# The same steps of an attention-and-MLP kernel in another written order

## The chip, the cores and the metric

The kernel runs on one core of a Trainium2 chip. The time is the device time of one launch, in microseconds (us), lower being better; where several runs were made, their median is given. A profiled execution, taken by the hardware profiler, gives the start and length of every instruction on the core's engines: TensorE (PE, with its weight loads as PEld), VectorE (DVE), ScalarE (ACT), GpSimd (POOL) and SyncE (SP), which here issues nearly all DMA transfers.

## The reference

Windowed attention with sink tokens, then a gated MLP. Shapes: 4 batches, 8 heads, 768 positions, head width 64; the MLP has 3072 tokens, width 512, inner width 1536. Inputs and output are float32.

```python
scores = scale * np.matmul(q, k.transpose(0, 1, 3, 2))
keep = (pos[None, :] < 4) | ((rel >= 0) & (rel < 128))     # 4 sinks, a window of 128
a = np.exp(np.where(keep, scores, -1e9) - max);  a = a / (sum(a) + 1e-9)
x = np.matmul(a, v).transpose(0, 2, 1, 3).reshape(B * S, H * D)
out = (np.maximum(x @ w_gate, 0.0) * (x @ w_val)) @ w_out
```

## The kernel before

The whole program is written out as a list of tokens, `ORDER`, and a loop at the end calls one small function for each token. A token is a name and its arguments: `G.0.1.5` is `up(0, 1, 5, 0)`. The order of the tokens is the order of the instructions in every engine's queue; the engines wait for each other through semaphores that follow from the data and from the buffers. There is no other loop over the work, so an order is a schedule.

The attention is done in 16 head pairs i, four to a batch (i = 4b to 4b+3). For each pair:

- `kl.i`, `ql.i` load k and q (384 KB each), for pair 0 in halves (`hk`, `hq`); `v.w.j` loads row block j (128 KB; 14 KB for j = 6) of the values of two pairs (w = i // 2). The values are read in pieces of 64 floats, 256 bytes.
- `kc`, `qc` on POOL, `kC`, `qC` on ACT (for halves `hc` and `hd` on POOL, `hC` and `hE` on ACT, `hD` on DVE) cast them to bf16. `c`, `cA` cast values, `f`, `fA` put the sink rows into them.
- For the first six pairs `TK`, `TQ` (halves: `HK`, `HQ`) turn k and q on TensorE, and copies on ACT (`ka`, `kb`, `qA`, `qB`, `ha`, `hX`) or DVE (`kd`, `ke`, `qa`, `qb`, `hg`, `hx`) bring them back; the later pairs are turned by DMA (`tk`, `tq`), and `od` on POOL copies shifted keys.
- `B` or `S` computes the scores of one of three groups g on TensorE, with 64 rows of the array for each of two heads (the form 64*128 in the profile, L411). For pairs 0 to 3 the mask is added by a matmul (`b`, L404), for the others a multiplication on DVE (`M`) applies it after `E`, the exponential on ACT (L426).
- `Vd` sums the exponentials over the keys on TensorE, in tiles of 32 columns (128*32, L445); `t`, `r`, `s`/`sa`, `R` bring the reciprocals into place (DVE, `sa` on ACT).
- `Va.i.part` is the output product on tiles of 64 columns (128*64, L454), and `x.i.part` on DVE writes its scaled result into `xT`, the MLP's input.

All other matmuls use the whole array (128*128). TensorE's form therefore changes whenever the order goes from one of these four kinds to another.

For each batch b the MLP runs over two column groups g (378 and 390 tokens) and 12 blocks m of the inner width: `G.b.g.m` and `W.b.g.m` (L507, 4 matmuls each) make gate and value, `u` on ACT applies the relu, `h` on DVE multiplies into `hT`. `F.b.t.m0.m1` (L529) is the output product of token tile t over blocks m0 to m1; `y` copies it out on ACT, `o` or `p` store it. `Z.3.5` does the last tile in three pieces. The weights are loaded in six chunks of 512 KB each: `gl.c`, `xl.c` (gate, value; blocks 2c and 2c+1) and `ol.c` (output), into six buffers used in turn; `gc`, `xc`, `oc` on POOL and `gC`, `xC`, `oC` on ACT cast a block (for `oc` a chunk), and a buffer is free again when both of its blocks are cast.

The eight PSUM banks are used as four pairs, given out in the order of the tokens by `take`, which picks the free pair that was used longest ago; a pair is free when the last user named has come (`use`). `N.n` and `P.n` (`spin4`, `spin`) are matmuls on zeros at the start that keep TensorE running while the first loads land. The order before does this from its first weights on:

```
S.4.1 gc.4 S.4.0 gc.5 x.2.0 E.4.0 Va.3.0 gC.2 R.3 x.3.0 Va.2.1 x.2.1 Va.3.1 xc.5 x.3.1 gl.0 S.4.2 G.0.0.4 E.4.2
G.0.0.2 E.4.1 xc.4 u.0.0.4 G.0.0.5 kl.5 u.0.0.2 u.0.0.5 gl.5 W.0.0.5 G.0.1.5 W.0.0.4 gc.3 M.4.1 gl.4 xC.2 h.0.0.5 xl.5
```

Lines that the change and the prediction touch:

```python
    30	ORDER = """
    93	F.3.3.8.12 y.3.4 y.3.3 o.3.2 o.3.3 o.3.4 Z.3.5
   578	        for token in ORDER:
   579	            name, *args = token.split(".")
   580	            OPS[name](*map(int, args))
```

Of the kernel before, what the change touches and what calls it, by code (L numbers as in the profile page):

```python
# [40 lines left out]
W.0.0.2 G.0.1.2 xC.0 gC.0 h.0.0.2 u.0.1.5 h.0.0.4 u.0.1.2 gc.11 W.0.1.2 v.3.1 W.0.1.5 h.0.1.2 xC.1 G.0.1.4 u.0.1.4  # L41
xc.3 v.2.0 gC.10 G.0.1.0 gc.9 G.0.1.3 h.0.1.5 W.0.1.4 u.0.1.0 W.0.1.0 h.0.1.0 u.0.1.3 G.0.0.3 G.0.0.11 xc.10 ql.5
W.0.0.3 h.0.1.4 kC.5 W.0.1.3 gC.1 TK.5 u.0.0.3 h.0.0.3 xl.4 G.0.0.0 h.0.1.3 kl.7 xl.3 ke.5 W.0.0.0 xC.11 u.0.0.11
W.0.0.11 qc.5 G.0.1.11 TQ.5 ka.5 h.0.0.11 G.0.1.1 v.2.6 gl.3 qb.5 qa.5 u.0.0.0 gC.8 ol.2 h.0.0.0 W.0.1.11 ql.6 W.0.1.1
S.5.2 u.0.1.1 u.0.1.11 h.0.1.11 xC.9 S.5.0 h.0.1.1 S.5.1 G.0.1.10 ol.5 E.5.2 M.4.2 G.0.0.8 M.5.2 E.5.0 E.5.1 W.0.1.10
G.0.0.10 G.0.1.9 W.0.1.9 xC.8 gc.6 u.0.1.10 xC.6 gc.7 u.0.1.9 W.0.0.10 u.0.0.10 h.0.1.9 h.0.1.10 G.0.0.1 kl.6 xc.7
oc.2 ol.1 h.0.0.10 W.0.0.1 ol.3 G.0.0.9 G.0.1.8 u.0.0.1 h.0.0.1 u.0.0.9 G.0.0.6 qc.6 u.0.0.8 ol.0 W.0.0.9 tq.6 oc.0
ql.7 W.0.0.8 ol.4 h.0.0.8 kC.6 tk.6 G.0.1.7 h.0.0.9 u.0.0.6 M.5.0 G.0.1.6 W.0.1.6 v.2.4 oC.1 M.5.1 W.0.0.6 W.0.1.8
u.0.1.6 h.0.0.6 G.0.0.7 h.0.1.6 oC.3 W.0.0.7 u.0.0.7 v.3.5 kc.7 u.0.1.7 M.4.0 cA.2.0.2 W.0.1.7 u.0.1.8 qc.7 oc.5
h.0.1.7 v.2.2 h.0.0.7 tk.7 Vd.4 Vd.5 v.3.4 od.6 t.2 tq.7 v.2.5 oC.4 v.2.3 od.7 F.0.0.0.8 F.0.1.0.8 S.6.1 h.0.1.8 v.3.0  # L50
# [566 lines left out]
```

## Time and profile before

| | |
|---|---|
| runs (3) | 243.02, 243.04, 244.06 us; median 243.04 |
| the profiled execution's own time | 243.59 us |
| its span, first to last instruction | 241.8 us |
| TensorE busy | 235.4 us, 97% |
| DVE, ACT, POOL busy | 132.4, 131.5, 57.4 us |
| gate and value products (L507) | 144.2 us of matmuls, 768 recorded |
| output product of the MLP (L529) | 60.7 us, 265 recorded |
| scores, sums, outputs of the attention | some 13.5, 10 and 12.1 us |
| HBM read and written | 28.43 and 6.29 MB |

A row of the profile's groups gives the line of the kernel, the engine, the operation, what it writes and reads, the shape, the number of instructions, their busy time, the mean of one, and the idle time of the engine ahead of them with what ended it. The ends of matmuls are modelled and overlap the next start, so the step from start to start is the time that a matmul takes in a stream. A few matmul records can be missing.

### The profile page before, as it was taken

The page shows a single profiled execution, that of the slowest core. Times are in us where ns is not written, and L with a number is a line of the kernel's source. Part 1 is how long each engine was busy: PE and PEld are TensorE (multiplying, and loading weights), DVE is VectorE, ACT ScalarE, POOL GpSimd, SP SyncE. Part 2 cuts the span into 40 slices and gives each one's busy share as a digit, 9 for nine tenths or more (in the row PEclk, how much of TensorE's full clock was granted, in tenths as well). Part 3 has the DMA queues.
Part 4 walks back from the last instruction along what each step waited for, and adds up shares of the span by engine and source line. Part 5 has one row for each costly group of instructions (what it writes and reads, how often), then busy time and mean ns, then how long its engine had stood idle before and what let it go on. Part 6 is the DMA issues. An engine that isn't in the chain of part 4 may idle for free.

```text
span 241.8 us, 4953 instructions
## 1 busy us (share of the span) xinstructions
PE 235.4 (97%) x1916; PEld 136.2 (56%) x1927; DVE 132.4 (55%) x268; ACT 131.5 (54%) x254; POOL 57.4 (24%) x106
## 2 busy tenths in 40 slices
PE   8999899999999999999999999999999999999995
PEld 2656556665546566556555565556574456655444
DVE  6599744737478635366888425397768034443100
ACT  2799877776495243596681163868650342432212
POOL 5467623323428043160103210230000000000000
PEclk9999999999999999999999999999999999999999
DMA  5999999999999999933986927140000180000033
GB/s 166 329 288 298 351 354 290 341 305 250 213 204 227 168 225 194 225 69 86 269 151 162 265 77 154 31 134 0 3 0 3 39 309 1 3 0 0 0 133 130
DMA packets 88327, 38.97 MB, mean 161 GB/s; under 512 B 73712, under 2 KB 83824, under 8 KB 88304
## 3 DMA queue, kind: packets, MB, share of 16 engines
q1 hardware_dynamic: 88160, 38.59, 64.4%
q8 instruction: 15, 0.25, 0.5%
q10 hardware_dynamic: 144, 0.07, 0.1%
q14 instruction: 8, 0.07, 0.1%
HBM read 28.43 MB, written 6.29 MB: 144 GB/s over the span
## 4 chain that ended last, share of the span: by engine, by line
PE 85%; DMA 5%; issue 5%; SPq 1%; ACT 1%; POOL 0%; DVE 0%; POOLq 0%
PE pp L507 52%; PE pp L529 21%; PE pp L454 3%; PE pp L411 3%; DMA ws<-in_moe_w_gate_dram 3%; DMA qf<-in_q_dram 2%; PE pp L445 2%; PE pp L189 2%; SPq L244 1%; PE pp L404 1%; PE pp L369 0%; ACT ee L426 0%; POOL qn L261 0%; PE pp L336 0%; ACT wg L277 0%
## 5 line engine op out<-in xcount | busy, mean ns | idle before, releaser
L519 DVE TENSOR_TENSOR hT<-gs,pp 128x378 bf16<-128x378 f32 (+1 forms) x96 | 50.7, 552 | 73.4 <-PE pp L507 51.6
L514 ACT ACTIVATE gs<-pp 128x378 f32<-128x378 f32 (+1 forms) x96 | 44.2, 494 | 53.9 <-PE pp L507 41.5
L507 PE MATMUL pp<-xT,wg 128*128 128x378 bf16 (+1 forms) x384 | 72.3, 326 | 0.4 <-ACT wg L277 0.4
L507 PE MATMUL pp<-xT,wv 128*128 128x378 bf16 (+1 forms) x384 | 71.9, 325 | 0.0
L529 PE MATMUL pp<-wo,hT 128*128 128x512 bf16 x265 | 60.7, 379 | 1.2 <-issue 1.0
L507 PEld LDWEIGHTS <-wv 128*128 128x128 bf16 x384 | 37.3, 98 | 25.3 <-issue 0.4
L507 PEld LDWEIGHTS <-wg 128*128 128x128 bf16 x384 | 36.8, 98 | 26.1 <-issue 1.0
L426 ACT ACTIVATE ee<-pp 128x1010 bf16<-128x1010 f32 (+2 forms) x48 | 44.0, 961 | 11.9 <-PE pp L411 11.7
L529 PEld LDWEIGHTS <-hT 128*128 128x128 bf16 x276 | 26.1, 98 | 30.4 <-issue 0.4
L535 ACT COPY ws<-pp 128x512 f32<-128x512 f32 x23 | 13.1, 590 | 26.8 <-PE pp L529 26.8
L432 DVE TENSOR_TENSOR ee<-ee,msk 128x1014 bf16<-128x1014 bf16 (+2 forms) x36 | 24.6, 716 | 3.3 <-ACT ee L426 2.9
L490 DVE STREAM_TRANSPOSE R<-r 128x832 f32<-128x832 f32 x16 | 16.4, 1037 | 5.2 <-ACT r L482 4.7
L496 DVE TENSOR_TENSOR xT<-pp,R 128x390 bf16<-128x390 f32 (+1 forms) x32 | 16.1, 543 | 3.9 <-PE pp L454 3.5
L269 POOL CAST vn<-vf 128x512 bf16<-128x512 f32 (+1 forms) x18 | 12.6, 721 | 23.1 <-DMA vf<-in_v_dram 23.1
L411 PE MATMUL pp<-qT,kE 64*128 64x255 bf16 (+4 forms) x164 | 13.5, 248 | 0.3 <-ACT qT L362 0.2
L454 PE MATMUL pp<-ee,vn 128*64 128x252 bf16 (+6 forms) x256 | 12.1, 242 | 0.0
L261 POOL CAST qn<-qf 128x768 bf16<-128x768 f32 x11 | 9.1, 828 | 12.7 <-DMA qf<-in_q_dram 12.4
L454 PEld LDWEIGHTS <-vn 128*64 128x64 bf16 x256 | 10.7, 110 | 1.8 <-issue 1.1
L297 POOL COPY kO<-kE 128x372 bf16<-128x372 bf16 x10 | 5.6, 563 | 25.5 <-PE pp L411 22.9
L258 POOL CAST kn<-kf 128x768 bf16<-128x768 f32 x11 | 9.0, 826 | 8.3 <-DMA kf<-in_k_dram 6.8
L465 DVE STREAM_TRANSPOSE t<-pp 128x832 f32<-128x832 f32 (+1 forms) x10 | 8.7, 868 | 4.2 <-PE pp L445 4.1
L411 PEld LDWEIGHTS <-kE 64*128 64x128 bf16 x164 | 6.8, 93 | 7.2 <-issue 5.1
(89 smaller groups left out, 140.8 us busy)
## 6 DMA issues: line engine op xcount, KB each, us to landing
vf<-in_v_dram SPq DMA_DIRECT2D x48, 128.0 KB, 4.2
kf<-in_k_dram SPq DMA_DIRECT2D x15, 384.0 KB, 5.3
qf<-in_q_dram SPq DMA_DIRECT2D x15, 384.0 KB, 5.7
out_dram<-ws SPq DMA_DIRECT2D x10, 512.0 KB, 3.4
ws<-in_moe_w_gate_dram SPq DMA_DIRECT2D x6, 512.0 KB, 6.4
ws<-in_moe_w_val_dram SPq DMA_DIRECT2D x6, 512.0 KB, 7.6
ws<-in_moe_w_out_dram SPq DMA_DIRECT2D x6, 512.0 KB, 5.1
out_dram<-ws SPq DMA_DIRECT2D x3, 256.0 KB, 2.0
```

Of the source, the lines that this page charges most:

```text
L269: copy(dst[:, j0:j1, :, :].rearrange("p j h d -> p (j h d)"), src[:, j0:j1, :, :].rearrange("p j h d -> p (j h d)"))
L411: mm = lambda h, c0, c1, lhs, rhs, st: on(("S", i, g), "PE", 1 << h, nc.tensor.matmul(out=ps[:, h, c0:c1], lhsT=lhs, rhs=rhs, start=st, st ...
L426: on(("S", i, g), "ACT", 3, nc.scalar.activation(ee[i % NE][:, g, :, 0:n], use(("S", i, g))[:, :, 0:n], Act.Exp, bias=0.0, scale=scale))
L432: nc.vector.tensor_tensor(x, x, msk[:, g, 0:n].unsqueeze(1).to_broadcast([128, 2, n]), op=Alu.mult)
L454: on(("V", i), "PE", 1 << part, nc.tensor.matmul(out=ps[64 * h:64 * h + 64, part, o0:o0 + c1 - c0], lhsT=vn[w % NVN][:, j, h0 + h, :], rhs ...
L490: nc.vector.transpose(out=R[:].rearrange("p s (c e) -> p (s c) e", e=32), in_=r.rearrange("p s c -> p (s c)").unsqueeze(2).to_broadcast([1 ...
L496: on(("V", i), "DVE", 1 << part, nc.vector.tensor_tensor(xT[b % 2][:, p, c0:c1], use(("V", i))[:, part, 0:c1 - c0], held_r[i][:, part, 0:c ...
L507: on(("F", b, g, m), "PE", 1 << which, nc.tensor.matmul(out=ps[:, which, 0:c1 - c0], lhsT=(wg, wv)[which][:, ko, m * 128:(m + 1) * 128], r ...
L514: on(("F", b, g, m), "ACT", 1, nc.scalar.activation(x[:, 0:n], use(("F", b, g, m))[:, 0, 0:n], Act.Relu, bias=0.0, scale=1.0))
L519: on(("F", b, g, m), "DVE", 2, nc.vector.tensor_tensor(hT[:, m, c0:c1], gs[b, g, m][:, 0:c1 - c0], use(("F", b, g, m))[:, 1, 0:c1 - c0], o ...
L529: on(name, "PE", 1 << t % 2, nc.tensor.matmul(out=ps[:, t % 2, :], lhsT=hT[:, m, t * 128:(t + 1) * 128], rhs=wo[:, m, :], start=m == 0, st ...
L535: on(name, "ACT", 1 << t % 2, act_copy(staged(b, t), use(name)[:, t % 2, :]))
```

## The change

Only `ORDER` is rewritten. The steps are the same except for which engine does some of the casts and copies: 53 of 1039 tokens are replaced by tokens for the same step on another engine, and `N.10` by `N.9`. The sequence of forms on TensorE is another (for instance `Va.0.0 Va.0.1 Va.1.0` together, and `Vd.10 Vd.11` together), the loads are asked for in another order, and `v.1.5`, `v.1.3`, `v.1.4` now all stand ahead of `gl.2`, which `xl.2`, `gl.1`, `xl.1`, `xl.0` follow. The core of the diff, the beginning and the stretch of the first MLP tiles and of the output weights:

```diff
 ORDER = """
-hk.0.0 sF sE N.10 sM hk.0.1 hq.0.0 mk.0 hc.0.0 mk.1 mk.2 hq.0.1 sI mb.1 b.0.1 mb.0 HK.0.0 hE.0.0 HQ.0.0 b.0.0 mb.2 P.3
-hD.0.1 kl.1 ql.1 v.0.0 v.0.6 hc.0.1 HK.0.1 kl.2 ql.2 HQ.0.1 v.0.2 ha.0.0 hx.0.0 hX.0.1 hg.0.1 B.0.0 b.0.2 B.0.1 B.0.2
...
-v.1.0 qB.3 t.0.1 B.2.1 r.0.1 v.1.2 b.3.0 b.3.2 kd.3 f.0.5 s.0.1 ke.3 qc.4 E.2.1 B.3.0 Vd.2 R.1 E.3.0 B.3.2 t.1.2 r.1.2
-c.1.0.2 gl.2 c.1.2.4 Va.0.0 E.3.2 f.1.3 Va.0.1 b.3.1 v.1.5 B.3.1 TK.4 v.1.4 TQ.4 Va.1.0 x.0.1 sa.1.2 gl.1 E.3.1 f.1.1
-x.0.0 c.1.4.7 f.1.5 qA.4 R.2 kb.4 x.1.0 Vd.3 t.1.3 P.2 r.1.3 ka.4 xl.2 xl.1 qB.4 Va.2.0 xl.0 Va.1.1 v.2.1 sa.1.3 x.1.1
-S.4.1 gc.4 S.4.0 gc.5 x.2.0 E.4.0 Va.3.0 gC.2 R.3 x.3.0 Va.2.1 x.2.1 Va.3.1 xc.5 x.3.1 gl.0 S.4.2 G.0.0.4 E.4.2
-G.0.0.2 E.4.1 xc.4 u.0.0.4 G.0.0.5 kl.5 u.0.0.2 u.0.0.5 gl.5 W.0.0.5 G.0.1.5 W.0.0.4 gc.3 M.4.1 gl.4 xC.2 h.0.0.5 xl.5
...
+sF sE hk.0.0 sI N.9 sM hq.0.0 hk.0.1 mk.0 mb.0 hq.0.1 mk.2 P.3 hC.0.1 kl.1 hc.0.0 ql.1 mk.1 HK.0.0 v.0.6 mb.1 b.0.0
+hd.0.1 kc.1 hD.0.0 HQ.0.0 HK.0.1 HQ.0.1 v.1.6 ql.2 kl.2 qc.1 P.2 b.0.1 kc.2 mb.2 v.0.3 hg.0.0 hX.0.0 hx.0.1 hg.0.1
+qc.2 B.0.0 b.0.2 E.0.0 B.0.2 B.0.1 TK.1 b.1.1 E.0.2 kd.1 TQ.1 v.0.0 qb.1 qa.1 kl.3 b.1.2 E.0.1 Vd.0 kb.1 B.1.2 v.0.2
+ql.3 v.1.2 kc.3 B.1.1 t.0.0 b.1.0 v.0.5 r.0.0 TK.2 c.0.2.4 B.1.0 kd.2 E.1.2 v.0.4 TQ.2 E.1.1 b.2.2 E.1.0 b.2.0 qa.2
+B.2.0 kl.4 ke.2 qc.3 c.0.4.7 f.0.5 Vd.1 v.0.1 s.0.0 qB.2 E.2.0 f.0.3 TK.3 v.1.1 v.1.0 B.2.2 kb.3 ql.4 t.0.1 b.3.2 R.0
+kd.3 TQ.3 b.2.1 c.0.0.2 E.2.2 f.0.1 kc.4 B.2.1 c.1.0.2 qA.3 qB.3 b.3.0 B.3.2 B.3.0 r.0.1 s.0.1 v.1.5 b.3.1 v.1.3 E.2.1
+f.1.1 R.1 Vd.2 qc.4 B.3.1 E.3.2 E.3.0 c.1.2.4 Va.0.0 Va.0.1 t.1.2 v.1.4 r.1.2 f.1.3 x.0.0 Va.1.0 x.0.1 gl.2 TK.4 E.3.1
+Vd.3 c.1.4.7 sa.1.2 kb.4 x.1.0 t.1.3 R.2 ka.4 xl.2 TQ.4 qA.4 f.1.5 Va.1.1 qB.4 Va.3.0 gl.1 Va.2.0 r.1.3 x.1.1 sa.1.3
+S.4.0 gc.4 gc.5 x.2.0 S.4.1 xc.4 E.4.0 xl.1 R.3 xl.0 kl.5 Va.2.1 Va.3.1 gc.2 S.4.2 x.3.0 xc.2 v.2.6 gl.0 x.2.1 G.0.0.4
+E.4.1 G.0.0.5 xC.5 x.3.1 G.0.1.5 M.4.1 u.0.1.5 W.0.1.5 xc.3 ql.5 W.0.0.5 h.0.1.5 gC.3 G.0.1.2 kc.5 u.0.0.5 h.0.0.5
+W.0.0.4 xl.4 u.0.1.2 gc.1 E.4.2 W.0.1.2 gl.5 G.0.1.4 h.0.1.2 gc.0 G.0.0.3 u.0.0.4 u.0.0.3 G.0.0.2 xc.0 xl.5 u.0.1.4
+gl.3 xc.1 gc.11 qC.5 u.0.0.2 xc.11 W.0.1.4 h.0.0.4 xC.9 TK.5 M.4.2 ke.5 W.0.0.2 W.0.0.3 h.0.1.4 h.0.0.3 gl.4 G.0.1.3
...
+kl.7 ol.5 G.0.1.11 u.0.1.3 u.0.1.0 h.0.0.0 G.0.0.11 u.0.0.11 h.0.1.3 xc.7 v.2.1 ol.3 kl.6 gc.8 W.0.0.11 ol.1 u.0.1.11
+W.0.1.11 G.0.1.1 ql.6 gc.9 h.0.1.0 gc.7 W.0.1.1 h.0.0.11 G.0.1.10 u.0.1.1 h.0.1.11 h.0.1.1 ol.0 S.5.2 E.5.2 S.5.1
+S.5.0 ol.2 W.0.1.10 E.5.1 G.0.0.1 u.0.1.10 W.0.0.1 G.0.0.8 u.0.0.1 W.0.0.8 E.5.0 kc.6 G.0.0.10 h.0.0.1 u.0.0.8 M.5.1
+ql.7 G.0.1.8 u.0.1.8 M.5.0 W.0.0.10 h.0.0.8 tk.6 G.0.1.9 W.0.1.9 u.0.1.9 M.5.2 oC.4 W.0.1.8 qc.6 h.0.1.10 G.0.1.7
...
 """.split()
```

More of the change, by code (lines that the diff above doesn't have):

```diff
@@ L41 @@
[L41 to L50, printed above, removed]
@@ new lines @@
+E.7.0 f.3.3 fA.2.1 M.7.2 ql.8 Va.5.0 M.7.0 M.7.1 v.4.0 c.3.0.2 Va.4.0 R.4 Va.4.1 y.0.2 y.0.3 Va.5.1 Vd.6 cA.3.4.7 Vd.7
+F.0.4.0.8 t.3 kl.10 f.3.1 f.3.5 v.5.2 x.4.0 F.0.5.0.8 Va.7.0 x.4.1 r.3 sa.3 x.5.1 Va.6.0 x.5.0 R.6 ql.10 Va.6.1 R.7
+qc.8 kl.9 kc.8 Va.7.1 F.0.5.8.12 x.7.1 y.0.5 x.6.1 F.0.4.8.12 G.1.1.11 tq.8 x.7.0 G.1.1.4 x.6.0 kc.9 y.0.4 v.5.3
+G.1.0.9 u.1.1.4 W.1.1.4 W.1.1.11 u.1.1.11 G.1.1.5 h.1.1.11 u.1.0.9 u.1.1.5 h.1.1.4 W.1.0.9 G.1.0.0 G.1.1.3 W.1.1.5
+v.4.1 W.1.1.3 W.1.0.0 v.4.3 h.1.1.5 u.1.0.0 G.1.0.7 W.1.0.7 ql.9 u.1.0.7 h.1.0.9 cA.4.0.2 h.1.0.7 ql.11 h.1.0.0
@@ new lines @@
+u.1.1.3 G.1.0.4 h.1.1.3 G.1.1.10 W.1.1.10 u.1.0.4 qC.9 kl.12 G.1.1.8 G.1.1.9 tk.8 u.1.1.9 W.1.1.9 W.1.0.4 v.4.2
+W.1.1.8 u.1.1.10 u.1.1.8 od.8 c.5.2.4 tq.9 h.1.0.4 tk.9 h.1.1.10 G.1.1.7 u.1.1.7 od.9 v.5.1 G.1.0.2 h.1.1.8 G.1.1.0
+W.1.1.7 W.1.1.0 W.1.0.2 h.1.1.9 u.1.1.0 u.1.0.2 h.1.1.7 h.1.1.0 S.8.2 S.8.1 S.8.0 v.5.0 qc.11 h.1.0.2 kC.10 v.5.4
+E.8.1 E.8.0 E.8.2 G.1.0.11 v.5.6 W.1.0.11 G.1.0.10 v.5.5 G.1.1.2 kl.11 tq.11 tk.10 W.1.0.10 u.1.0.11 W.1.1.2 u.1.1.2
+h.1.0.11 qc.10 tq.10 c.4.2.4 u.1.0.10 h.1.0.10 S.9.2 M.8.2 h.1.1.2 E.9.2 S.9.1 S.9.0 G.1.1.1 E.9.0 G.1.0.1 ql.12
@@ new lines @@
+Va.14.0 sa.7 Va.13.0 x.13.0 Va.13.1 x.12.1 x.13.1 x.12.0 Va.15.0 Va.14.1 R.15 R.14 Va.15.1 x.14.1 F.2.4.0.8 x.14.0
+F.2.2.0.8 F.2.5.0.8 x.15.0 F.2.5.8.12 G.3.0.4 x.15.1 u.3.0.4 W.3.0.4 G.3.0.5 h.3.0.4 F.2.2.8.12 u.3.0.5 G.3.1.1
+W.3.0.5 F.2.3.0.8 h.3.0.5 y.2.2 W.3.1.1 u.3.1.1 F.2.3.8.12 y.2.5 h.3.1.1 G.3.1.0 G.3.1.8 y.2.3 F.2.4.8.12 G.3.1.4
+u.3.1.8 p.2.0 y.2.4 W.3.1.8 W.3.1.0 G.3.1.2 W.3.1.4 u.3.1.2 u.3.1.0 p.2.1 W.3.1.2 h.3.1.0 G.3.0.10 h.3.1.8 h.3.1.2
+G.3.0.3 u.3.0.10 G.3.0.1 W.3.0.1 u.3.1.4 u.3.0.3 W.3.0.3 u.3.0.1 h.3.0.1 G.3.0.0 W.3.0.10 h.3.0.3 u.3.0.0 h.3.1.4
@@ L94 @@
+F.3.3.0.8 F.3.3.8.12 y.3.4 o.3.4 y.3.3 o.3.3 Z.3.5
 """.split()
```

77 lines of the change are left out of this document (31 added, 46 removed).

## The prediction

> **What bounds the kernel now.** I read the page first, then TensorE's waits, its timeline around the first gate product, the chain of waits, and ACT's timeline in the same place.
>
> ```profile
> span 241.8 us, 4953 instructions
> PE 235.4 (97%) x1916; PEld 136.2 (56%) x1927; DVE 132.4 (55%) x268; ACT 131.5 (54%) x254; POOL 57.4 (24%) x106
> PE   8999899999999999999999999999999999999995
> ```
>
> TensorE is busy 97%; every other engine has room. A busy share can hide waits, so the waits of TensorE after 27.97 us come next:
>
> ```profile
> PE pp L529 <- issue: 1.0, 6, 0.2
> PE pp L507 <- ACT wg L277: 0.4, 1, 0.4
> ```
>
> The six "issue" gaps are not idle time: the page has 276 weight loads of L529 and only 265 matmuls, and before each such gap one load stands without its matmul. The records are missing, the array was working. So after 27.96 TensorE never waits, and this part of the time is a plain sum of matmuls. Only two things can change it: what a change of tile form costs, and new waits. What lies ahead of 27.96 is another matter:
>
> ```profile
> 26.46 0.35 PE L411 MATMUL pp<-qT,kE 64*128 64x255 bf16 x6
> 26.75 0.81 PE L507 MATMUL pp<-xT,wg 128*128 128x378 bf16 x4
> 27.96 1.55 PE L507 MATMUL pp<-xT,wg 128*128 128x378 bf16 x8 [0.40 <-ACT wg L277]
> ```
>
> G.0.0.4 starts at 26.75 and holds TensorE 0.64 us (the step from tile to tile in the steady part), so G.0.0.2 could start at 27.39. It starts at 27.96: 0.57 us lost (0.40 by the modelled ends). The chain says to what:
>
> ```profile
> 20.30 6.97 DMA ws<-in_moe_w_gate_dram
> 27.26 0.02 issue
> 27.29 0.63 ACT wg L277
> 27.91 0.05 issue
> ```
>
> G.0.0.2 needs the second gate chunk (gl.1), issued at 20.30, landed at 27.26, cast by ACT (gC.2). So the present kernel is a prologue, bound by loads and by ACT, whose useful end is 27.96 - 0.64 = 27.32, and then an unbroken TensorE stream.
>
> **The forms.** A change of form is seen in start times:
>
> ```profile
> 113.84 1.44 PE L507 MATMUL pp<-xT,wv 128*128 128x378 bf16 x8
> 115.22 0.28 PE L411 MATMUL pp<-qT,kE 64*128 64x253 bf16 x2
> ...
> 115.94 0.90 PE L445 MATMUL pp<-ee,ones 128*32 128x127 bf16 x32
> 116.77 1.04 PE L529 MATMUL pp<-wo,hT 128*128 128x512 bf16 x3
> ```
>
> Two W tiles take 2 x 0.64 = 1.28 us in the stream; here 115.22 - 113.84 = 1.38, so entering the score form costs 0.10. Two sums (L445, 128*32) followed by one another step 0.38 each; 116.77 - 115.94 = 0.83, so leaving costs 0.07. By the same subtraction everywhere: sums to outputs (128*64) 0.09, outputs to sums 0.08, outputs to full 0.08, full to sums or outputs 0.09. I counted the changes in both orders along TensorE's queue from G.0.0.4 on: 44 before, 40 after. Three fewer sums to outputs, and one fewer each of outputs to sums, outputs to full and full to sums; one more each of sums to full and full to outputs. Sum: 3 x 0.09 + 0.08 + 0.08 + 0.09 - 0.08 - 0.09 = 0.35 us less, all on the path. Ahead of G.0.0.4 it is 30 against 29, beside waits, so nothing.
>
> **The first weights.** Before, gl.2 is the 25th load and gl.1 has v.1.5 and v.1.4 ahead of it. After, two more value loads (256 KB together) stand ahead of gl.2, and then come xl.2, gl.1, xl.1. TensorE uses gl.2 for three tiles (G.0.0.4, G.0.0.5, G.0.1.5), then xl.2 for two, and needs gl.1 only with the sixth tile, 3.2 us after the first. So gl.1 stops being the gate; gl.2 is. What two value loads cost:
>
> ```profile
> 16.00:18.00 2.00, 2.00 (x22) 1.06 (x21) 1.91 (x9) 1.98 (x5) 2.00 (x5) 1.00 1.05 243
> 24.00:27.00 3.00, 2.68 (x52) 2.13 (x48) 2.86 (x6) 2.33 (x7) 2.33 (x4) 1.00 1.01 344
> ```
>
> The last column is GB/s: 243 while mostly values move, 344 while weights alone do. 0.262 MB at 243 is 1.1 us. The median weight load of a gate takes 6.4 us to land; gl.2 was issued at 17.84, so now it lands at 17.84 + 1.1 + 6.4 = 25.3. Its casts gc.4 and gc.5 (0.61 each, POOL) end at 25.9 and 26.5, in time for a G.0.0.4 at 26.4 and a G.0.0.5 at 27.1. The ends: before, gc.4 started at 25.62 without waiting, so gl.2 had landed by then; plus 1.1 is 26.7 at the latest, or 24 at the earliest. xl.2 takes gl.1's place in bytes (27.26): cast 27.9, wanted at 28.4. gl.1 takes xl.2's (28.5, from the wait that ended at 28.56): cast 29.2, wanted at 29.7. Both fit with 0.5 us.
>
> The Trainium skill, "DMA: Bandwidth & Descriptors", Specifications, speaks against this part: pieces under 512 B do not move at line rate. The values are read in pieces of 256 B, and the two rows agree with it (243 against 344). By byte count at 344 the two loads would have cost 0.8 us, by the rule the 1.1 of the row.
>
> **What sets G.0.0.4 then.** S.4.2 follows E.4.0, and G.0.0.4's last matmul needs x.3.0.
>
> ```profile
> 18.96 1.78 ACT L426 ACTIVATE ee<-pp 128x1010 bf16<-128x1010 f32 x2 [0.17 <-PE pp L411]
> 20.91 0.84 ACT L482 COPY r<-r 32x13 f32<-32x13 f32 x4 [0.18 <-DVE r L470]
> 25.39 1.02 ACT L426 ACTIVATE ee<-pp 128x1010 bf16<-128x1010 f32 x1
> ```
>
> From E.1.0 (14.10) to the end of E.4.0 (26.41) ACT is nearly solid: its steps, plus about 0.8 us of waits (0.17 and 0.18 as shown, with the 0.1 of overlap that each breaks, and two of 0.1 at E.2.2 and E.2.0). After, ka.2 leaves ACT ahead of E.1.0, which can start when E.1.1 lets it, 13.65; qB.2 (0.38) and kb.3 (0.42) come in. Adding the measured steps of the new queue (E 0.90, 0.92 or 0.75 by width, query copies 0.38, r's copies 0.86, key copies 0.42 and 0.51) gives 12.19 us, so E.4.0 ends at 25.84 with no wait, at 26.4 if as much is waited as now. I take 26.1: the scores now come in the order in which ACT reads them, but kl.2 lands behind ql.2, so TK.2 moves from 12.19 to 12.8. G.0.0.4 follows 0.34 us after E.4.0, as now: 26.2 to 26.75, and not before 26.37 by DVE (R.3 after sa.1.3, 1.04, then x.3.0 0.55, wanted 0.48 after G starts). Take 26.5: 0.8 us earlier than 27.32. One spin fewer (0.43 at the cold pace of 427 ns a matmul) saves nothing: TQ.1 waits for qc.1 and so for ql.1, landed at 9.37, in both.
>
> **New waits in the stream.** The old order is tight: some fifteen times after 28 us TensorE starts a tile within 0.2 us of the copy or multiply that frees its bank (G.0.0.8 0.10 after E.5.2, G.2.0.10 0.06 after E.14.0, both net of the 0.05 of a semaphore). The new order has as many such places, others (G.0.0.10 behind E.5.0, G.1.1.2 behind E.8.0, S.9.0 behind h.1.0.10). Each can cost 0 to 0.1; I allow 0.1 in all, ends 0 and 0.8. Two queues are passed by moved steps. On SP, xl.4 now stands ahead of gl.5, xl.5, gl.3, gl.4 and xl.3, and waits for the buffer that xc.3 frees, at about 31.1 (xl.1 lands at 29.82, then gc.2's turn is over and xc.2, xc.3 take 0.6 each); until then kl.5, gl.0 and ql.5 (1.3 MB, 3.8 us at 344) are still moving behind xl.0 (31.21), so the transfers do not stop, and gl.5 lands near 38, wanted cast at 40.2. On POOL, kc.5 stands ahead of gc.1 and gc.0 and waits for kl.5: its place in bytes lies 0.4 of the way from xl.0 (31.21) to the old kl.5 (33.98), 32.3; cast 33.1, TK.5 wants it at 34.3. Both are hidden by over 1 us; gone, each us of lateness is one of TensorE's. ACT, DVE and POOL do the same work in sum, a few casts change engine, and all are at 24 to 55%.
>
> Sum: -0.8 - 0.35 + 0.1 = -1.05 us. The profiled run took 243.59 (span 241.8, 1.79 around it), so it would be 242.5; the median of the runs shown is 0.55 lower, 243.04, and I forecast from it: 242.0.
>
> **Rivals.** *The first weights gate as before.* gl.1 needed 3.0 us more than the value load ahead of it (24.24 to 27.26) for 512 KB; if gl.2, now in that place, does the same, gc.4 ends at 27.9 and G.0.0.4 starts at 27.95, 0.63 late: 243.04 + 0.63 - 0.35 = 243.3. Against it, gl.2 itself did not drag before.
>
> *The prologue closes up fully*: ACT waits for nothing, no new waits: G.0.0.4 at 26.37 or a little under, 243.04 - 0.95 - 0.35 = 241.7, and 241.3 if DVE's chain moves up with the earlier sums.
>
> *Slower: the output weights come late.* ol.2 is now asked for last of the six, and F.0.0.0.8 needs it with its fifth matmul, 34.5 us after G.0.0.4, at 61.0; before, the last was ol.4, which F.0.0.0.8 does not read. At the place in bytes before, ol.0 landed at 57.5; 256 KB more makes 58.4, the cast (1.04) 59.4. If the transfers from 44.63 on (the landing of xl.3, 4110 KB ahead of ol.2's place) run at the 233 GB/s of the stretch from 54 to 60 instead of 313 to 340, those 4.2 MB land at 62.7, the cast ends at 63.7, and TensorE stands 2.7 us: 244.7. It decides from a landing after 60.0.
>
> *Many small waits*: 0.8 instead of 0.1: 242.7.
>
> *The clock.* TensorE's clock was granted from 6.96 us: the steps are 427 ns for 512 columns before, 216 after. If the changed start (spin, then products that wait for casts) lets it come one stretch later, the some 2.7 us of matmuls up to TQ.1 double; 0.6 of it falls into present waits, leaving 2 us: 244.0. The Trainium skill, "TensorE: Matmul & The Clock Gate", Part 1, says the clock opens after a busy window of some 3.4 us that runs free, and one spin fewer speaks against the change by that rule. But in the rows TensorE is solid from 1.06 on, and by the landings it stays so, which is why this gets little.
>
> **Chances.** Forecast (241.6 to 242.4) 0.52; first weights gate 0.15; prologue closes up 0.16; small waits 0.06; output weights 0.08; clock 0.03. About 0.5% (1.2 us, so 241.8 and 244.3) can be told from no change here. Faster: the 0.16 and some 0.22 of the forecast's 0.52, 0.38. Slower: output weights and part of the clock, 0.10. The rest, 0.52, is within. The range for 8 in 10 goes from 241.1 (prologue closed up, with 0.2 for the median) to 243.7 (first weights gate, with some small waits).
>
> **What would show it.** Right: no TensorE wait on wg at L507 or only a trace of it, G.0.0.4 at 26.2 to 26.8 followed at once by five tiles; 40 changes behind it; from it to the last product 0.35 us less. The step on the first weights is wrong if the chain still has a DMA of w_gate just ahead of the first product; the step on ACT if E.4.0 ends after 26.5; the one on new waits if TensorE's waits after 28 us, missing records apart, exceed 0.3 us.

## The result, and the profile after

The changed kernel takes 244.01 us (median of 22 runs, 243.14 to 245.43); the kernel before took 243.33 in as many runs beside it (242.67 to 244.06). The ratio is 1.0033, with a 95% interval of 1.002 to 1.0046: a little slower, above the range of the prediction. The three runs from whose median, 243.04, the forecast was made lie 0.3 us under the median of the 22. The profiled execution took 243.85, with the same span as before.

From the page of the changed kernel:

```profile
span 241.8 us, 4948 instructions
PE 233.9 (97%) x1914; PEld 135.2 (56%) x1926; DVE 131.9 (55%) x274; ACT 127.6 (53%) x242; POOL 61.2 (25%) x112
PE   8798999999999999999999999999999999999994
```

By this row TensorE is busy 1.5 us less, and the span is the same. Some ten matmul records are missing in each page (e2 and e1 below have all 1927 and 1926, and 235.4 and 235.0 us), so the row can't be read that finely. TensorE's waits in the changed kernel after 27 us:

```profile
PE pp L552 <- ACT ws L535: 0.7, 1, 0.7
PE pp L529 <- issue: 0.2, 1, 0.2
```

The second is a missing record. The wait on the gate weights (L507 on wg, 0.4) is gone, and a wait has come up at L552, which is `Z.3.5`, the last tile of the kernel. The timeline of the changed kernel there (start, length, engine, line, operation):

```profile
235.46 0.59 ACT L535 COPY ws<-pp 128x512 f32<-128x512 f32 x1 [1.03 <-PE pp L529]
236.10 2.81 PE L552 MATMUL pp<-wo,hT 128*128 128x256 bf16 x36 [0.67 <-ACT ws L535]
```

and of the kernel before:

```profile
236.12 2.81 PE L552 MATMUL pp<-wo,hT 128*128 128x256 bf16 x36
236.31 0.59 ACT L535 COPY ws<-pp 128x512 f32<-128x512 f32 x1 [0.28 <-PE pp L529]
```

Before, Z starts 0.2 us ahead of `y.3.3`, ACT's copy of the last output product, and runs beside it. After, the last product ends 0.7 to 0.85 us earlier, but Z starts only behind the end of that copy, 236.05. In these two executions it gives back all that was won.

The reason stands in `close`. It puts Z's three pieces on three of the four PSUM pairs, counted from the pair of `F.3.4`, whatever these hold:

```python
   550	            ps = PP[(owner[name] + 1 + c) % 4]
```

`F.3.4` has pair 2 in both orders, so the pieces go to pairs 3, 0, 1. In the old order pair 3 holds `F.3.0` and `F.3.1`, copied out long before, and `F.3.3` is on pair 0. In the new order `F.3.3` is on pair 3: in its second bank, while Z's piece writes the first. But Z's matmuls don't go through `on`, the helper that declares two banks of a pair independent, and so the first piece waits for the copy.

The start, in TensorE's timeline of the changed kernel:

```profile
26.60 0.36 PE L411 MATMUL pp<-qT,kE 64*128 64x255 bf16 x6 [0.47 <-ACT ee L426]
26.89 2.11 PE L507 MATMUL pp<-xT,wg 128*128 128x378 bf16 x12
28.84 1.46 PE L507 MATMUL pp<-xT,wv 128*128 128x390 bf16 x8
```

Three gate tiles and two value tiles in a row from 26.89, with no wait: 0.43 us ahead of the useful 27.32 of before. From there to the point at which Z could begin it is 0.35 to 0.43 us less than before's 208.80, with 40 changes of form for 44. So by these two profiles: start -0.43, forms -0.35 to -0.43, wait at the end +0.75 to 0.85, and equal spans.

### The profile page after: what moved, and what is told of

The parts are those of the page before. It is cut to its first block, busy times and chain, and to the rows that moved or that the text cites. A ratio compares the mean times of both kernels' runs of the same rounds, so it can differ in the third digit from the quotient of the medians.

```text
span 241.8 us, 4948 instructions
## 1 busy us (share of the span) xinstructions
PE 233.9 (97%) x1914; PEld 135.2 (56%) x1926; DVE 131.9 (55%) x274; ACT 127.6 (53%) x242; POOL 61.2 (25%) x112
## 4 chain that ended last, share of the span: by engine, by line
PE 89%; DVE 4%; DMA 2%; ACT 1%; issue 1%; SPq 1%; POOL 0%; DVEq 0%
PE pp L507 52%; PE pp L529 25%; PE pp L411 4%; PE pp L454 3%; PE pp L445 2%; DMA qf<-in_q_dram 2%; PE pp L552 1%; DVE R L490 1%; ACT ee L426 1%; DVE xT L496 1%; DVE t L465 1%; PE pp L336 1%; SPq L238 1%; DVE r L484 1%; PE pp L404 0%
## 5 line engine op out<-in xcount | busy, mean ns | idle before, releaser
L519 DVE TENSOR_TENSOR hT<-gs,pp 128x390 bf16<-128x390 f32 (+1 forms) x96 | 50.3, 552 | 73.4 <-PE pp L507 49.4
L507 PE MATMUL pp<-xT,wg 128*128 128x378 bf16 (+1 forms) x384 | 72.4, 326 | 0.0
L507 PE MATMUL pp<-xT,wv 128*128 128x378 bf16 (+1 forms) x384 | 71.9, 325 | 0.0
L529 PE MATMUL pp<-wo,hT 128*128 128x512 bf16 x264 | 62.0, 379 | 0.7 <-issue 0.2
L507 PEld LDWEIGHTS <-wv 128*128 128x128 bf16 x384 | 37.4, 98 | 25.2 <-issue 0.2
L507 PEld LDWEIGHTS <-wg 128*128 128x128 bf16 x384 | 36.8, 98 | 25.7 <-issue 0.8
L529 PEld LDWEIGHTS <-hT 128*128 128x128 bf16 x276 | 26.1, 98 | 30.4 <-issue 0.8
L432 DVE TENSOR_TENSOR ee<-ee,msk 128x1014 bf16<-128x1014 bf16 (+2 forms) x36 | 25.7, 744 | 8.5 <-ACT ee L426 8.5
L258 POOL CAST kn<-kf 128x768 bf16<-128x768 f32 x12 | 10.7, 888 | 30.1 <-DMA kf<-in_k_dram 18.1
L496 DVE TENSOR_TENSOR xT<-pp,R 128x378 bf16<-128x378 f32 (+1 forms) x32 | 15.7, 542 | 1.0 <-PE pp L454 0.7
L411 PE MATMUL pp<-qT,kE 64*128 64x255 bf16 (+4 forms) x164 | 13.0, 248 | 0.5 <-ACT ee L426 0.5
L454 PEld LDWEIGHTS <-vn 128*64 128x64 bf16 x256 | 10.6, 110 | 1.9 <-issue 1.7
L454 PE MATMUL pp<-ee,vn 128*64 128x252 bf16 (+6 forms) x256 | 11.6, 242 | 0.0
```

Of the source, the lines that this page charges most:

```text
L411: mm = lambda h, c0, c1, lhs, rhs, st: on(("S", i, g), "PE", 1 << h, nc.tensor.matmul(out=ps[:, h, c0:c1], lhsT=lhs, rhs=rhs, start=st, st ...
L432: nc.vector.tensor_tensor(x, x, msk[:, g, 0:n].unsqueeze(1).to_broadcast([128, 2, n]), op=Alu.mult)
L454: on(("V", i), "PE", 1 << part, nc.tensor.matmul(out=ps[64 * h:64 * h + 64, part, o0:o0 + c1 - c0], lhsT=vn[w % NVN][:, j, h0 + h, :], rhs ...
L496: on(("V", i), "DVE", 1 << part, nc.vector.tensor_tensor(xT[b % 2][:, p, c0:c1], use(("V", i))[:, part, 0:c1 - c0], held_r[i][:, part, 0:c ...
L507: on(("F", b, g, m), "PE", 1 << which, nc.tensor.matmul(out=ps[:, which, 0:c1 - c0], lhsT=(wg, wv)[which][:, ko, m * 128:(m + 1) * 128], r ...
L519: on(("F", b, g, m), "DVE", 2, nc.vector.tensor_tensor(hT[:, m, c0:c1], gs[b, g, m][:, 0:c1 - c0], use(("F", b, g, m))[:, 1, 0:c1 - c0], o ...
```

## Experiments

All times are medians of interleaved runs; "span" is the median span of the same runs; the ratio is to the kernel before on the same chip, whose medians beside them were 243.59 us (span 241.8) for the runs e, 243.55 (241.75) for g, 243.36 (241.55) for h and 243.44 (241.7) for i.

| run | what differs | us | span | ratio, 95% interval |
|---|---|---|---|---|
| e1_tail_pair | changed order, Z on other pairs | 242.99 | 241.1 | 0.998 (0.9966 to 0.9994) |
| e2_before_tail_wait | order before, Z's first piece on F.3.3's pair | 244.46 | 242.65 | 1.004 (1.0025 to 1.0055) |
| e3_new_start | new start, old rest | 244.92 | 243.1 | 1.005 (1.0027 to 1.0073) |
| e4_old_start | old start, new rest, no wait at the end | 243.18 | 241.3 | 0.9985 (0.9967 to 1.0003) |
| g_changed | the changed order again (11 of 12 runs; one took 306.6) | 243.74 | 241.8 | 1.0019 (0.9998 to 1.004) |
| g_forms | e1 with 64 changes of form for 40 | 246.12 | 244.2 | 1.0113 (1.0095 to 1.0132) |
| g_qc4 | e1 with qc.4 earlier on POOL | 243.02 | 241.1 | 0.998 (0.9966 to 0.9994) |
| g_before_tiles | order before, G.0.0.2 sixth | 244.34 | 242.6 | 1.0055 (1.0032 to 1.0077) |
| h_pool, h_act, h_dve | e1 with an idle copy on one engine | 243.33, 243.14, 243.23 | 241.35, 241.3, 241.25 | 0.999, 0.9991, 0.9992 (each within 0.0017) |
| h_gl2 | e1 with gl.2 ahead of three values | 243.34 | 241.5 | 1.0002 (0.9983 to 1.002) |
| i_bank | changed order, banks of Z's pair declared independent | 243.06 | 241.05 | 0.9982 (0.9964 to 1.0001) |

Two theories stood at the start: *tail*, that the wait of Z.3.5 is what the change lost, and *prologue*, that the new start is late in most runs and the profiled one was lucky.

### The pair of the last tile

```diff
-            ps = PP[(owner[name] + 1 + c) % 4]
+            ps = PP[(owner[name] + 2 + c) % 4]
```

In the changed order (e1_tail_pair) this takes the first piece off the pair of `F.3.3`:

> The changed order; only the pairs of PSUM banks that the three pieces of Z.3.5 are put on differ: 0, 1, 2 in place of 3, 0, 1, so that the first piece no longer shares a pair with F.3.3, which y.3.3 is still copying out. Theory 'tail': the first L552 follows F.3.3.8.12 without a wait, at 235.3 in place of 236.1, and the time falls by 0.7 to 0.85 us, from 244.0 to 243.2-243.3. Rival 'prologue': the changed order loses its time before G.0.0.4, and the wait at the end covers something that ends late anyway (the stores): within 0.2 us of the changed order, 243.8 to 244.2.

In the order before (e2_before_tail_wait) the same edit puts it there:

> The order of before; only the pairs of the three pieces of Z.3.5 differ: 0, 1, 2 in place of 3, 0, 1, which here puts the first piece on the pair of F.3.3. Theory 'tail': L552 waits for y.3.3, which ends at 236.9, and starts there in place of 236.12: 0.75 to 0.85 us longer, 244.1 in place of 243.3. Rival 'prologue': no difference over 0.2 us.

The timelines of e1_tail_pair and then of e2_before_tail_wait:

```profile
235.31 2.81 PE L552 MATMUL pp<-wo,hT 128*128 128x256 bf16 x36
235.51 0.58 ACT L535 COPY ws<-pp 128x512 f32<-128x512 f32 x1 [1.03 <-PE pp L529]
```

```profile
236.36 0.59 ACT L535 COPY ws<-pp 128x512 f32<-128x512 f32 x1 [0.28 <-PE pp L529]
237.00 2.81 PE L552 MATMUL pp<-wo,hT 128*128 128x256 bf16 x36 [0.68 <-ACT ws L535]
```

Both came out as *tail* says, on either side, though the times themselves lie off the expected ones (242.99 for 243.2 to 243.3, 244.46 for 244.1): the changed order loses the wait and 0.7 us of median span (241.1 against 241.8 in g_changed, on another chip), the old one gains it and 0.85. With the wait gone the changed order is faster than before by 0.2% (0.06 to 0.34), and this is the version that beats both.

### Bank or pair

In e1 the two engines also work on different pairs, so it doesn't tell whether the copy and the matmuls are in each other's way within a pair or are only kept apart by the program. i_bank keeps pairs 3, 0, 1 and declares the banks independent:

```diff
-            ps = PP[(owner[name] + 1 + c) % 4]
+            owner["Z", c] = (owner[name] + 1 + c) % 4
+            ps = PP[owner["Z", c]]
             for m in range(FM):
-                nc.tensor.matmul(out=ps[:, 0, 0:c1 - c0], ...
+                on(("Z", c), "PE", 1, nc.tensor.matmul(out=ps[:, 0, 0:c1 - c0], ...
```

> The changed order with its pairs 3, 0, 1 for Z.3.5, but the matmuls of Z go through the helper that tells the program that two uses of different banks of a pair do not depend on each other. The first piece writes bank 0 of pair 3, y.3.3 reads bank 1. Theory 'the wait is made by tracking the pair as one buffer': it goes, L552 starts at 235.3 as with other pairs, 243.0 (0.85 under the changed order). Rival 'ACT's reading and TensorE's writing get in each other's way in the pair': the start moves forward but the matmuls or the copy stretch beside each other, and less than half of it is won, 243.5 or more.

Its timeline (the matmuls of Z are on line 553 there):

```profile
235.36 2.81 PE L553 MATMUL pp<-wo,hT 128*128 128x256 bf16 x36
235.56 0.58 ACT L535 COPY ws<-pp 128x512 f32<-128x512 f32 x1 [1.03 <-PE pp L529]
```

The matmuls write bank 0 of pair 3 while ACT copies bank 1, the copy takes 0.58 as before, and the wait is gone. So it was made by following the pair as one buffer. The Trainium skill, "Perfetto Trace Analysis", Optimizing Tensor Performance, asks for independent groups to go round the PSUM banks so that one is copied out beside the next one's matmuls. The trace agrees once the program knows the banks apart, as the two rows of i_bank show; in the changed order the group was on another bank and waited 0.67 us all the same.

### The start and the rest taken apart

e3_new_start and e4_old_start join the two orders: one up to an early tile, and from there the steps still missing, in the sequence of the other.

```diff
 e3: ORDER = new order up to G.0.0.2, then the remaining steps in the old order
 e4: ORDER = old order up to W.0.0.5, then the remaining steps in the new order
```

> The order of before up to W.0.0.5 (the fifth tile of TensorE's stream), and from there all other steps in the changed order, with its 40 changes of form. The first piece of Z.3.5 falls on a pair that nobody is reading, since the pairs are dealt out in turn from the start. Theory 'tail': only the forms are left of the change, 0.35 us under before, 243.0. Rival 'prologue', by which the old start is the better one: 243.0 as well, but then the run with the new start is slower than this one. If new small waits in the stream eat the forms' gain: 243.3.

> The changed order up to G.0.0.2 (the eleventh tile of TensorE's stream), and from there all other steps in the order of before (its 44 changes of form, its last products). The first piece of Z.3.5 falls on a pair that nobody is reading. Theory 'tail', by which the new start is worth the 0.43 us that its profile shows: G.0.0.4 near 26.9, 0.4 us under before, 242.9. Rival 'prologue', by which the new start is late in most runs and loses 0.3 or more: 243.6 or above, with a wider scatter than before.

e4 has the forms of the change and nothing else of it, and takes 0.4 us less than before (0.5 by span), where 0.35 was worked out; its interval reaches from 0.8 us less to 0.1 more. e1, with the new start as well, is only 0.2 us faster than e4 by either measure, less than either interval.

e3 says nothing of the start. Its waits on TensorE are of its own making:

```profile
PE pp L507 <- ACT gs L514: 1.4, 1, 1.4
PE pp L507 <- ACT wv L277: 0.9, 1, 0.9
```

They lie at 40.4 and 36.2 us, where the casts and loads of the two orders don't fit together. Its start was at 27.06, near that of the changed order.

The changed order once more, on the chip of the other g runs:

> The changed order as it is, on the same chip as the three runs beside it. Theory 'tail and start': new start -0.2 to -0.4, forms -0.35, wait at the end +0.75 to 0.85; 0.0 to 0.3 us above before. Rival 'something else costs as well', by which the first comparison (0.7 above before) is the true size: 0.6 or more above before.

It is 0.2 us above before by the medians, 0.05 by span and 0.46 by the ratio: the size that the three parts give. The first comparison had 0.7 by the medians and 0.8 by the ratio, with a span of 242.05 against 241.55 to 241.8 for before in the runs here. The two intervals overlap; why the first came out higher is open.

### What the old start had waited for

The prediction's first gain was the wait of `G.0.0.2` for gl.1. g_before_tiles takes that tile from second to sixth place and leaves the loads alone:

```diff
-... G.0.0.4 E.4.2 G.0.0.2 E.4.1 xc.4 u.0.0.4 G.0.0.5 kl.5 u.0.0.2 u.0.0.5 gl.5 W.0.0.5 G.0.1.5 W.0.0.4 ...
+... G.0.0.4 E.4.2 E.4.1 G.0.0.5 G.0.1.5 xc.4 u.0.0.4 kl.5 u.0.0.5 gl.5 W.0.0.5 W.0.0.4 G.0.0.2 u.0.0.2 ...
```

> The order of before with one part of the change alone: G.0.0.2, the first tile that reads gl.1, goes from second to sixth place in TensorE's stream, behind G.0.0.5, G.0.1.5, W.0.0.5 and W.0.0.4; the loads stay in their order. (The end keeps its free pair.) Theory 'gl.1 gates every run by about 0.57 us': 0.5 us under before. Rival 'the gate of the profiled run is a draw of the landing times': 0 to 0.25 us under before, or 0.1 to 0.3 above, if the wait goes over to xl.2, which lands behind gl.1 here and is now wanted 0.6 us earlier than gl.1's second tile.

It is 0.8 us slower, for a reason that neither theory had. ACT's queue in g_before_tiles:

```profile
30.73 0.49 ACT L514 ACTIVATE gs<-pp 128x378 f32<-128x378 f32 x1 [1.36 <-PE pp L507]
31.11 1.13 ACT L277 CAST wv<-ws 128x512 bf16<-128x512 f32 x2
31.78 0.81 PE L507 MATMUL pp<-xT,wv 128*128 128x378 bf16 x4 [1.08 <-ACT wv L277]
```

The relu of the moved tile stands on ACT ahead of the cast `xC.2`; the tile went back and its relu with it. ACT stood idle 1.36 us for that relu's tile, and the cast behind it, whose row shows no wait for a load, came so late that `W.0.0.2` waited 1.08 us for it. As a test of the gate the run is spoilt. But together with e2 and e4 it holds three more executions of the same old start and the same loads, and ACT's cast `gC.2`, which needs gl.1 landed and ACT free, gives a bound on the landing. Before, e2_before_tail_wait, e4_old_start, g_before_tiles:

```profile
27.29 0.62 ACT L277 CAST wg<-ws 128x512 bf16<-128x512 f32 x1 [0.88 <-DMA ws<-in_moe_w_gate_dram]
```

```profile
26.66 0.62 ACT L277 CAST wg<-ws 128x512 bf16<-128x512 f32 x1
```

```profile
26.55 0.62 ACT L277 CAST wg<-ws 128x512 bf16<-128x512 f32 x1
```

```profile
26.35 0.62 ACT L277 CAST wg<-ws 128x512 bf16<-128x512 f32 x1
```

Only in the profiled execution of before did ACT wait for the load. In the three others gl.1 was there by the time ACT was free, at least 0.6 to 0.9 us earlier, and TensorE had no wait on gate weights (in e2 it waited 0.3 us for value weights a little later). The 0.57 us was one draw of the landing times, one in four executions.

### What a change of form costs

g_forms is e1 with seven groups of three score products pulled apart: where the order allows it one of a group goes a full tile earlier and one a full tile later.

```diff
-G.0.1.10 ... S.5.2 E.5.2 S.5.1 S.5.0 ... W.0.1.10
+S.5.2 E.5.2 G.0.1.10 ... S.5.1 ... W.0.1.10 S.5.0
```

> The changed order with the end mended (pieces of Z.3.5 on pairs 0, 1, 2), and seven of its groups of three score products pulled apart: one of the group goes one full tile earlier, one a full tile later. That makes 64 changes of tile form behind G.0.0.4 in place of 40, and no work more. Theory 'a change costs 0.08 to 0.10 us on the path': 24 x 0.09 = 2.2 us over the mended order, 245.1 (between 244.9 and 245.5). Rival 'the order's 0.35 us came from elsewhere, a change is hidden by the weight loads beside it': 243.0, at most 243.5.

TensorE's timeline in g_forms, and in the changed kernel:

```profile
43.64 0.82 PE L507 MATMUL pp<-xT,wv 128*128 128x390 bf16 x4
44.39 0.35 PE L411 MATMUL pp<-qT,kE 64*128 64x255 bf16 x6
44.68 0.83 PE L507 MATMUL pp<-xT,wg 128*128 128x390 bf16 x4
45.45 0.39 PE L411 MATMUL pp<-qT,kE 64*128 64x255 bf16 x4
45.77 0.83 PE L507 MATMUL pp<-xT,wv 128*128 128x390 bf16 x4
46.54 0.39 PE L411 MATMUL pp<-qT,kE 64*128 64x253 bf16 x4
46.86 0.33 PE L507 MATMUL pp<-xT,wg 128*128 128x378 bf16 x1
```

```profile
43.83 0.82 PE L507 MATMUL pp<-xT,wv 128*128 128x390 bf16 x4
44.49 0.82 PE L507 MATMUL pp<-xT,wg 128*128 128x390 bf16 x4
45.25 0.81 PE L411 MATMUL pp<-qT,kE 64*128 64x255 bf16 x14
45.98 0.83 PE L507 MATMUL pp<-xT,wv 128*128 128x390 bf16 x4
```

Three tiles and three products take 46.86 - 43.64 = 3.22 us pulled apart. Together they take 45.98 - 44.49 = 1.49 for one tile and the group, and 2 x 0.66 for the two other tiles, 2.81. Four more changes: 0.41 us, 0.10 each. From the first gate product to Z it is 211.74 in g_forms against 208.37 in e1; of these 3.37 us the 24 changes make 24 x 0.105 to 0.115, 2.5 to 2.8, and two new waits (L454 for a value cast 0.4, L445 for a mask multiplication 0.2) the rest. The median is 3.1 us over that of e1, above the theory's range for both reasons, and the rival is out. The Trainium skill, "TensorEngine Tiling (Array Packing)", Key Properties, says that a change of tiling mode drains TensorE; the trace agrees, and puts the price at a tenth of a microsecond here.

### What the new start waits for

The new start was to bring 0.8 us. In the traces the first gate product starts no earlier than with the old one: at 26.62 to 27.06 us in six executions with the new start (the changed order 26.89, e1 26.94, e3 27.06, g_changed 26.62, g_forms 26.70, i_bank 26.99), and at 26.66 to 26.98 in the four with the old one (before 26.75, e2 26.98, e4 26.86, g_before_tiles 26.66). What the new start saves is a wait in the first four tiles, which the old one had in two of its four executions (0.57 us in before, 0.30 in e2) and the new one in none (at most 0.17, in e3). By the medians of e1, e4 and before this is worth 0.2 to 0.35 us, less than the intervals of these runs.

In the changed kernel ACT sets the first gate product, as the prediction had it. TensorE's row and ACT's:

```profile
11.68 0.54 PE L445 MATMUL pp<-ee,ones 128*32 128x127 bf16 x16 [0.23 <-ACT ee L426]
12.55 2.66 ACT L426 ACTIVATE ee<-pp 128x814 bf16<-128x814 f32 x3 [0.49 <-PE pp L411]
25.54 1.92 ACT L426 ACTIVATE ee<-pp 128x1010 bf16<-128x1010 f32 x2
```

`E.1.2`, the first of the three at 12.55, waits 0.49 us for its scores: on TensorE the sums `Vd.0` (L445) stand ahead of those scores and wait themselves for ACT's `E.0.1`. From 12.55 to the end of `E.4.0` at 26.56 ACT doesn't wait at all. (The chain of waits names DVE just ahead of ACT's last copy of r, but ACT's rows show no idle time there.) The prediction's 13.65 for `E.1.0` is the old start of `E.1.2`, 11.98, and two steps of 0.75 and 0.92; `E.1.0` came at 14.20. From there ACT took 12.36 us, where 12.19 had been worked out without a wait.

Being earlier there doesn't help for long. In e1 `E.1.2` starts at 12.12, and ACT loses that again on the copies of pair 4's queries:

```profile
23.84 0.86 ACT L362 COPY qT<-pp 128x384 bf16<-128x384 bf16 x2 [0.39 <-PE pp L336]
```

They wait for `TQ.4`, and that for POOL's cast `qc.4`; `E.4.0` starts at 25.59. g_qc4 moves that cast ahead of two value casts:

```diff
-kc.4 B.2.1 c.1.0.2 ... f.1.1 R.1 Vd.2 qc.4
+kc.4 qc.4 B.2.1 c.1.0.2 ... f.1.1 R.1 Vd.2
```

> The changed order with the end mended, and one step moved: the cast qc.4 (GpSimd, 0.84 us) stands right behind kc.4, ahead of the value casts c.1.0.2 and f.1.1 (0.66 us together). Theory 'the new start hangs on GpSimd': qc.4 ends 0.66 us earlier, TQ.4 and the query copies on ACT follow, E.4.0 ends 0.4 us or so earlier, at 26.2, and G.0.0.4 starts near 26.5: 242.6. Rival 'ACT itself, or DVE's chain to x.3.0, is as late': no more than 0.15 us, 242.9; or slower, if Va.2.0 now waits for c.1.0.2.

POOL's row for qc.4 in g_qc4:

```profile
21.86 0.83 POOL L261 CAST qn<-qf 128x768 bf16<-128x768 f32 x1 [0.76 <-DMA qf<-in_q_dram]
```

The rival was right: the median is that of e1. The cast starts 0.57 us earlier than in e1 (22.43), not 0.66, since it now waits for its load, and ACT waits for it no more. But in this execution `E.1.2` started only at 12.60, and with no wait from there on ACT comes to `E.4.0` at 25.89. The value casts moved back are late for the output products as well: L454 waits 0.26 us on POOL at 24.30.

The next three runs put one copy of 128 x 507 bf16 that nobody reads into the queue of one engine (0.60 us on POOL, 0.62 on ACT, 0.71 on DVE by their rows):

```diff
+        "z": lambda: gp_copy(idle[:], mb[:, 1, 0:507]),      # h_act: act_copy, h_dve: dve_copy
-f.0.1 kc.4          -E.3.1 ... sa.1.2 kb.4          -t.1.3 R.2
+f.0.1 z kc.4        +E.3.1 ... sa.1.2 z kb.4        +t.1.3 z R.2
```

> The mended order with one idle step more: GpSimd copies 128 x 507 bf16 into a tile that nobody reads, just ahead of kc.4. It asks what the start of the gate products is worth to GpSimd's queue. Theory 'the new start hangs on GpSimd' (value casts, kc.4 and qc.4 in a row, for which TQ.4 and ACT wait): the copy's whole length, some 0.4 to 0.6 us, is added: 243.4 to 243.6. Rival 'only ACT sets it', as the prediction's step had it: under 0.15 us, 243.0 to 243.1.

> The mended order with the same idle copy on ACT, just ahead of kb.4. Theory 'the new start hangs on GpSimd': ACT waits 0.4 us for TQ.4 right behind kb.4 and ka.4 and takes the copy (some 0.5 us) up in that: 0 to 0.15 us, 243.0 to 243.1. Rival 'ACT sets it': the copy's whole length, 243.4 to 243.5.

> The mended order with the same idle copy on DVE, just ahead of R.2. DVE's chain R.2, x.1.1, R.3, x.3.0 ends beside E.4.0. If DVE is as tight as ACT, the copy's length (0.2 to 0.5 us) less 0.15 to 0.2 of slack: 243.1 to 243.3; with real slack on DVE 243.0.

Set against before on the same chip, the mended order stands at -0.60 (e1) and -0.38 (i_bank), the three at -0.03, -0.22 and -0.13: about 0.45 us more for POOL, 0.27 for ACT, 0.35 for DVE. Each run's interval is about 0.4 us to either side, so by the medians neither the sequence of the three is shown nor, for ACT and DVE, that there is a loss. h_dve came out as one of its theories had it; h_pool and h_act fell between theirs. The traces show where a copy is paid. `E.4.0` started between 25.27 and 25.70 in the six executions of the new start; in h_pool, h_act and h_dve (line numbers are one higher there):

```profile
24.34 0.86 ACT L363 COPY qT<-pp 128x384 bf16<-128x384 bf16 x2 [0.72 <-PE pp L337]
26.09 1.92 ACT L427 ACTIVATE ee<-pp 128x1010 bf16<-128x1010 f32 x2
```

```profile
25.85 1.92 ACT L427 ACTIVATE ee<-pp 128x1010 bf16<-128x1010 f32 x2
```

```profile
24.96 0.84 ACT L483 COPY r<-r 32x13 f32<-32x13 f32 x4 [0.43 <-DVE r L471]
25.83 1.92 ACT L427 ACTIVATE ee<-pp 128x1010 bf16<-128x1010 f32 x2
```

With the copy on POOL, ACT waits longer for the turned queries than in e1; with the copy on DVE it waits for the reciprocals; with the copy on ACT it doesn't wait, and the copy takes the place of e1's wait of 0.39 us and some more. So POOL and DVE reach the start through ACT, and each has only a few tenths to spare. POOL in its turn works without a break from the landing of a value load on:

```profile
17.99 0.83 POOL L270 CAST vn<-vf 128x768 bf16<-128x768 f32 x1 [2.07 <-DMA vf<-in_v_dram]
```

Last, the part of the change that has the weights asked for behind the values, undone:

```diff
-v.1.5 b.3.1 v.1.3 ... v.1.4 ... gl.2
+gl.2 v.1.5 b.3.1 v.1.3 ... v.1.4
```

Besides `v.1.5` and `v.1.4` this puts `v.1.3` behind `gl.2`, which in the order before stood ahead of it.

> The mended order with a part of the change undone: gl.2 is asked for ahead of v.1.5, v.1.3 and v.1.4, as before, in place of behind them. 512 KB at 300 to 340 GB/s move those values back by 1.5 to 1.7 us. Theory 'values first is right, since GpSimd's value casts stand ahead of what E.4.0 and x.3.0 need': c.1.4.7 waits for v.1.4, Va.1.1 and the x steps come late, G.0.0.4 0.5 to 1.5 us later, 243.5 to 244.5. Rival 'the loads of that stretch have slack': no difference over 0.15 us, 243.0.

POOL's value cast and TensorE's gate tiles in h_gl2:

```profile
24.55 0.61 POOL L269 CAST vn<-vf 128x512 bf16<-128x512 f32 x1 [1.38 <-DMA vf<-in_v_dram]
27.74 0.49 PE L507 MATMUL pp<-xT,wg 128*128 128x378 bf16 x2
```

The values come 1.4 us late for POOL, and in this execution the gate products start at 27.74, 0.8 us later than in e1. Over the runs it is 0.4 us by span, 0.35 by time, between what the two theories had and inside the intervals. The trace speaks for asking for the values first with the order of tiles that the change has; the medians don't settle it.

## Why the prediction was wrong

**New waits in the stream: the step that failed.** The prediction took 0.1 us, with ends at 0 and 0.8, and looked for them at places where a tile starts close behind what frees its bank. There were none of those: from 26.89 to the last `F` TensorE doesn't wait. One wait, 0.67 us in TensorE's row and 0.75 to 0.85 on the time, came at a place that was never looked at, the last tile, because the trace of before shows no wait there. What was needed stood in the rows of before: `y.3.3` runs from 236.31 to 236.90 beside Z's first piece, so that an order in which the two meet on one pair costs 236.95 - 236.12 = 0.8 us; and `close` counts its pairs without asking who holds them. The rival of many small waits had the size, 0.8, by luck: it was one wait, in another place.

**The first weights: half right.** gl.1 gates nothing any more, and five tiles follow each other. But the 0.57 us that this was to bring had been read from one profiled execution, and in three other executions of the old start that wait was not there. The casts of gl.2 ended at 25.9 and 26.5 as worked out (25.91 and 26.47), and that was luck: gl.2 was issued at 19.93, not at 17.84, and the casts didn't wait for it but for POOL, which came to them at 25.31. The start was to gain 0.8; against the useful 27.32 the profile shows 0.43, and the medians of e1, e4 and before 0.2 to 0.35, not clear of their noise.

**What sets G.0.0.4: the right engine, too early by 0.4.** The prediction had ACT, with E.4.0 ending at 26.1; it ended at 26.56, past the 26.5 that the prediction itself had set as a sign. The sum of ACT's steps held (12.36 us against 12.19, with no waits). The failed term is its beginning: E.1.0 was put at 13.65 by the old time of E.1.2 and came at 14.20, since the new order makes E.1.2 wait 0.49 us behind Vd.0. That POOL and DVE are nearly as late, so that little would have been won by a better beginning, the prediction had for DVE but not for POOL.

**The forms: right.** 0.35 us were worked out for four changes less; the profile shows 0.35 to 0.43, e4_old_start 0.4 (with an interval that reaches zero), and g_forms a price of 0.10 to 0.115 each. (The sum takes 0.08 for sums to full, where its own row gave 0.07; it changes nothing.)

**The queues passed, the output weights, the clock: right.** Neither xl.4 nor kc.5 held anything up, there is no wait on output weights, and the granted clock came no later than before in the profiled execution (from 5.5 us, against 6.96).

The sum with what the runs showed: -0.2 to -0.35 for the start, -0.35 to -0.4 for the forms, +0.85 for the last tile, and some 0.1 to 0.17 outside the span (below): +0.2 to +0.45 us, where -1.05 had been forecast. Measured were +0.2 and +0.7 by the medians, +0.46 and +0.8 by the ratios; what the larger of these hold beyond the sum is open.

## What to carry to other kernels

When an order of steps changes, the buffers that a fixed rule gives out change hands too, and a step that waited for nothing may then share a buffer with its neighbour: look at the last steps first, where a wait has nothing behind it that could hide it. A wait on a load that one profile shows is one draw; before it is counted as a gain, it should be seen in a second execution, or its slack bounded by the spread of landing times. If two banks are followed as one buffer, a free bank is no use until the program is told so.

## What the runs showed of the hardware

The same loads in the same order landed 0.9 us apart or more from one execution to the next (gl.1, the four casts above). That may be part of what spreads the runs of one kernel over 2.4 us of span (240.5 to 242.9 in 28 runs of before).

The time outside the span is not the same for all orders: 1.78 to 1.82 us on average for the kernels that end in the old order (before, e2, e3, g_before_tiles) and 1.89 to 2.0 for those that end in the new one (1.98 for the changed order, 1.91 for e1 and e4). It goes with the second half, whatever the start. What makes it was not tried.
